# Two-branch long convolution on one core: P rows in two buffers, phases on ScalarE, one reader per PSUM tile, and another order

## The chip, the cores and the metric

The kernel runs on one core of a Trainium2 chip. The metric is the device time of one execution in microseconds. The kernel before took 277.68 us as the median of three runs (277.12 to 280.39). The profile is of one execution of its own, which took 277.69 us; its span from the first to the last recorded instruction is 275.8 us.

The engines are named as in the profile: PE is TensorE (matmuls), PEld its weight loads, DVE is VectorE, ACT is ScalarE, POOL is GpSimd, SP is SyncE, which issues most transfers.

## The reference

L is 2048 positions, D is 448 channels, N is 256 modes. Branch A is a state-space convolution whose kernel K is made from complex exponentials; branch B is a short filter of four taps, a product with v, and a long convolution with a given kernel. The output mixes both branches by a gate g, one number per position.

```python
def _A_ref(u, A_re, A_im, B_re, B_im, C_re, C_im, log_dt, Dskip):
    dt = jnp.exp(log_dt)[:, None]
    ...
    P = jnp.exp(logdA[:, :, None] * l[None, None, :])
    K = jnp.einsum("dn,dnl,dn->dl", Cc, P, dB).real
    ...
    y = irfft2(rfft2(pad(u)) * rfft2(pad(K)))[..., :L]
    return y + u * Dskip

def _B_ref(q, k, v, shift_k, ssm_k, ssm_D):
    ...
    k_shift = k_shift + k_pad[:, t:t + S, :] * shift_k[:, ks - 1 - t]   # t = 0..3
    kv = k_shift * v
    y = irfft2(rfft2(pad(kv)) * rfft2(pad(ssm_k)))[:S] + kv * ssm_D
    return q * y

x = A_u
g = _sigmoid((x * gate_w).sum(-1, keepdims=True))
a = _A_ref(x, A_A_re, A_A_im, A_B_re, A_B_im, A_C_re, A_C_im, A_log_dt, A_Dskip)
b = _B_ref(x, B_k, B_v, B_shift_k, B_ssm_k, B_ssm_D)
return g * a + (1 - g) * b
```

(The transforms are abridged: pad, rfft2 and irfft2 stand for what the reference spells out with axes and types.)

## The kernel before

**Convolution by transforms on TensorE.** Channels go in four chunks H = 0 to 3 of 4 x 28 channels. For each chunk and branch a sequence is brought into transformed form in two steps: `spread` (PSUM tiles ps_c, copied to a tile zs or, for branch A's kernel, zsK) and `transform` (PSUM tiles ps, copied back over zs). `swapped` makes zsS, zs with its two halves of partitions exchanged, by two transfers on SP's queue. `products` multiplies zsS and zs by the transformed kernel on VectorE. `stage_a` (PSUM ps_a, copied to U) and `stage_b` (PSUM ps_b) transform back. Nearly every copy out of PSUM is a ScalarE instruction (`evac`); `evac_two`, used in the last step, gives every second one to VectorE. zs, zsS, zsK, U and others share a pool of NBQ = 7 buffers under the tag "q". Three PSUM buffers "ps" of two banks each serve spread, transform, stage_a and stage_b.

**The kernel K of branch A** is made in eight blocks j = 0 to 7, two per chunk. `Tables.levels` and `Tables.reals` fill a table ET (its parts are called EQ and EP): magnitudes by Exp, phases as integers (ks_ph) by a multiply and add on VectorE, then Sin on ScalarE, a product of the two, and for some entries a negation, on ScalarE for EQ's and on VectorE for EP's. Exp and Sin lie in different table sets, so ScalarE loads a table between them (ACT_TABLE_LOAD). `KGen.q_rows` builds 32 Q rows per chunk (kg_TQ). `KGen.block` builds P rows in the tile kg_TP: rows 0 to 15 by doublings (`mult` into kg_P, `add` back into kg_TP) and rows 16 to 31 as mirrored rows (`back`). For rows 8 to 15 one half of the product is written to kg_TP and the other to kg_P, and a transfer on GpSimd's queue with an accumulate adds them. TensorE then multiplies Q and P rows into the one PSUM tile pk; ScalarE copies it to kg_S; `gather` (PSUM ps_g, copied to kg_KT) puts the taps in order, and spread brings them into zsK.

**The opening.** Modes (A, B, C, four tables) are loaded and multiplied by the step size dt (ks_dt) on TensorE (ps_m). ScalarE copies the exponents into the tile early, where hold keeps, interleaved in one tile per half, two exponents and the coefficients; VectorE makes the coefficients (ks_tC_re, ks_tC_im, early). `save` writes them to memory (xfd), from where each later chunk loads its part (ks_xf). The four taps of branch B run as matmuls of k, transposed while loading, with diagonal matrices (front); VectorE multiplies the result (ps_v) into vt. `stage_b` of the constants fills sb_G in four pieces (phases sb_ph on VectorE, Sin on ScalarE, 16 products on VectorE). `sk_cols` adds dB to the first column of the loaded kernel skraw, on GpSimd.

**The steps.** `step` runs over the sequence B0, B1, A0, B2, A1, none, A2, B3; in each, a new chunk's spread and transform, the former's stage_a and stage_b, and one block. In the end come A's chunk 3, block 7, `mix` (weighings by the gate, gb and og), `transform_half` and `stage_a_half` in halves, and `epilogue_A`, which multiplies by the gate, adds (ept, vt) and stores.

**The order.** No engine call is made when the code meets it. The class Order records each, and `issue` makes them in the order of the list ORDER, each tied behind the one before it on the same engine. So every engine's order is that of the list, while semaphores keep data dependencies. As all are issued by one line, the profile gives nearly everything the same line (L148); groups are told apart by tiles.

```python
    def issue(self):
        last, done = {}, 0
        for run in ORDER.split():
            a, _, b = run.partition("-")
            for f, args, kw in self.calls[int(a):int(b or a) + 1]:
                ins = f(*args, **kw)
                engine = str(ins.ins.engine)
                if engine in last:
                    after(self.tc, ins, last[engine])
                last[engine] = ins
```

Of the kernel before, what the change touches and what calls it, by code (L numbers as in the profile page):

```python
# [9 lines left out]
ACT = mybir.ActivationFunctionType  # L10
ALU = mybir.AluOpType
# [6 lines left out]
P = 128  # L18
# [20 lines left out]
NBQ = 7  # L39
# [312 lines left out]


def transform_half(nc, psum, W, zs, evac, half):
    for kk in range(2):
        pt = psum.tile([P, 2, 512], f32, name="ps_2", tag="ps")
        for i in range(16):
            k = 16 * kk + i
# [686 lines left out]
```

## Time and profile before

| | |
|---|---|
| median of three runs | 277.68 us |
| the profiled execution | 277.69 us |
| its span | 275.8 us |
| granted TensorE clock, mean | 0.956 |
| DVE busy | 241.7 us, 488 instructions |
| ACT busy | 226.7 us, 383 instructions |
| PE busy | 210.7 us, 5770 matmuls |
| POOL busy | 15.9 us |
| transfers | 24.74 MB, mean 90 GB/s |

The page's strip of the span in 40 equal slices, 6.9 us each; a digit is the busy share in tenths:

```profile
PE   0610958879988799798997789867887999699830
DVE  7599899999989799979996899899999997967950
ACT  2795696999899999998998799999999989546400
POOL 8000000000400000100010001001001001000000
PEclk9999999999999899998998999999999999979975
```

A row of a group reads: line, engine, operation, written tile <- read tiles, sizes, count, then busy us, mean ns of one, and the idle time of the engine just before them with what ended it. A row of the timeline reads: start, length, engine, instruction, count, and in brackets how long the engine had been idle and what it waited for. In the table of waits, the numbers are us in total, times, and the longest.

### The profile page before, as it was taken

Reading aid. Unit: us, or ns where it says so; the run is one execution under the profiler, and the core shown is the slowest. Engines: PE = TensorE matmul, PEld = TensorE weight load, DVE = VectorE, ACT = ScalarE, POOL = GpSimd, SP = SyncE. Lnnn points to the kernel's source line nnn. Section 1 sums busy time; section 2 is a strip of 40 time slices with the busy share of each in tenths; the row PEclk is TensorE's granted clock in tenths of the full one; section 3 lists DMA queues with packets and bytes.
Section 4 is the critical chain, followed back from the end, with each engine's and each line's share of the span. In section 5 each row is a group of like instructions: output and inputs, shape, how many; then the busy total and the mean of one; then the engine's idle time right before and its main releaser. Section 6 shows DMA issues by size and latency. Waiting matters only on the chain.

```text
span 275.8 us, 12739 instructions
## 1 busy us (share of the span) xinstructions
PE 210.7 (76%) x5770; PEld 193.3 (70%) x5770; DVE 241.7 (88%) x488; ACT 226.7 (82%) x383; POOL 15.9 (6%) x51
## 2 busy tenths in 40 slices
PE   0610958879988799798997789867887999699830
PEld 0500858877887798687995779766886899688820
DVE  7599899999989799979996899899999997967950
ACT  2795696999899999998998799999999989546400
POOL 8000000000400000100010001001001001000000
PEclk9999999999999899998998999999999999979975
DMA  7999799607804500390093019003042263600077
GB/s 149 224 204 172 131 235 175 99 1 153 118 5 91 116 5 4 83 186 5 5 209 47 5 50 199 10 2 70 6 90 64 54 138 60 147 5 2 2 141 127
DMA packets 55110, 24.74 MB, mean 90 GB/s; under 512 B 49680, under 2 KB 52368, under 8 KB 55056
## 3 DMA queue, kind: packets, MB, share of 16 engines
q1 hardware_dynamic: 48640, 19.34, 37.7%
q0 software_dynamic: 1152, 3.67, 7.2%
q10 hardware_dynamic: 5264, 0.92, 2.1%
q8 instruction: 45, 0.74, 1.2%
q14 instruction: 9, 0.07, 0.1%
HBM read 7.95 MB, written 2.87 MB: 39 GB/s over the span
## 4 chain that ended last, share of the span: by engine, by line
ACT 38%; PE 29%; DVE 15%; DMA 9%; issue 5%; SPq 0%; DVEq 0%; POOL 0%; POOLq 0%; ACTq 0%
ACT zs L148 15%; ACT ET L148 7%; ACT U L148 6%; DMA kg_TP<-kg_P 6%; PE pk L148 5%; PE ps_a L148 5%; PE ps L148 5%; PE ps_c L148 5%; PE ps_b L148 5%; ACT zsK L148 5%; DVE vt L148 2%; DVE scratch L148 2%; PE ps_g L148 2%; PE ps_gate L148 2%; DMA skraw<-in_B_ssm_k_dram 2%
## 5 line engine op out<-in xcount | busy, mean ns | idle before, releaser
L148 ACT CAST zs<-ps 128x896 bf16<-128x896 f32 x48 | 44.0, 944 | 1.0 <-PE ps L148 0.6
L148 ACT CAST zs<-ps_c 128x1024 bf16<-128x1024 f32 (+1 forms) x48 | 42.7, 937 | 1.3 <-PE ps_c L148 1.2
L148 PEld LDWEIGHTS <-front 128*32 128x32 bf16 (+1 forms) x496 | 19.1, 159 | 27.3 <-issue 22.3
L148 PEld LDWEIGHTS <-s_W 128*128 128x128 bf16 x544 | 28.9, 100 | 12.7 <-issue 9.6
L148 PE MATMUL pk<-kg_TP,kg_TQ 128*32 128x32 bf16 x1792 | 33.2, 242 | 5.1 <-issue 2.9
L148 PEld LDWEIGHTS <-kg_TQ 128*32 128x32 bf16 x1792 | 31.2, 160 | 7.0 <-issue 4.8
L148 PE MATMUL ps_a<-sa_R,zs 128*128 128x128 bf16 x224 | 32.7, 235 | 0.3
L148 ACT CAST U<-ps_a 128x1024 bf16<-128x1024 f32 (+1 forms) x30 | 27.2, 936 | 6.9 <-PE ps_a L148 6.7
L148 PE MATMUL ps_b<-U,sb_G 128*128 128x28 bf16 x1024 | 29.5, 175 | 4.1 <-issue 1.4
L148 PE MATMUL ps_a<-sa_R,zsS 128*128 128x128 bf16 x224 | 32.1, 232 | 0.5 <-DVE zsS L148 0.5
L148 PE MATMUL ps<-zs,s_W 128*128 128x112 bf16 x384 | 27.7, 220 | 5.5 <-ACT zs L148 4.2
L148 PEld LDWEIGHTS <-sb_G 128*128 128x128 bf16 x1024 | 27.8, 96 | 5.8 <-issue 3.2
L148 DVE TENSOR_TENSOR kg_TP<-kg_TP,ET 128x1792 bf16<-128x1792 bf16 x24 | 26.1, 1090 | 5.8 <-DMA kg_TP<-kg_P 5.0
L148 PEld LDWEIGHTS <-zsS 128*128 128x128 bf16 x224 | 29.6, 152 | 1.3 <-DVE zsS L148 0.7
L148 PEld LDWEIGHTS <-zs 128*128 128x128 bf16 x224 | 29.4, 151 | 0.8
L148 PE MATMUL ps_v<-front 128*32 128x336 bf16 (+3 forms) x448 | 16.0, 310 | 16.0 <-DVE front L148 13.1
L148 ACT ACTIVATE ET<-ks_ph 128x448 bf16<-128x448 int16 x40 | 23.2, 602 | 4.1 <-DVE kg_P L148 2.6
L148 DVE TENSOR_TENSOR kg_TQ<-kg_TQ,ET 128x896 bf16<-128x896 bf16 (+1 forms) x36 | 24.8, 730 | 0.0
L148 DVE TENSOR_TENSOR kg_P<-kg_TP,ET 128x1792 bf16<-128x1792 bf16 (+1 forms) x24 | 22.4, 934 | 0.1
L148 PE MATMUL ps_c<-Wc,uu 128*64 128x128 bf16 x224 | 18.4, 290 | 1.6 <-ACT U L148 0.6
L148 PE MATMUL ps_c<-Wc,vt 128*64 128x128 bf16 x224 | 17.1, 285 | 1.4 <-ACT zs L148 1.2
L148 PEld LDWEIGHTS <-uu 128*64 128x64 bf16 x224 | 16.5, 210 | 2.4 <-issue 1.5
(102 smaller groups left out, 427.4 us busy)
## 6 DMA issues: line engine op xcount, KB each, us to landing
zsS<-zs SPq DMA_DIRECT2D x16, 448.0 KB, 5.7
kg_TP<-kg_P POOLq DMA_DIRECT2D x8, 448.0 KB, 5.7
vt<-in_B_v_dram SPq DMA_DIRECT2D x4, 448.0 KB, 6.8
skraw<-in_B_ssm_k_dram SPq DMA_DIRECT2D x16, 112.0 KB, 4.8
uu<-in_A_u_dram SPq DMA_DIRECT2D x4, 448.0 KB, 8.5
ks_xf<-xfd SPq DMA_DIRECT2D x3, 336.0 KB, 3.3
out_dram<-vt ACTq DMA_DIRECT2D x8, 112.0 KB, 3.8
out_dram<-vt SPq DMA_DIRECT2D x8, 112.0 KB, 3.6
```

Source lines behind the costliest of these rows:

```text
L148: ins = f(*args, **kw)
```

## The change

The change has these parts:

1. P rows: a tile kg_TP of 48 rows is allocated once. Even blocks use rows 0 to 15 as their first rows, odd blocks rows 32 to 47; the mirrored rows 16 to 31 are shared. Where rows come in another order, matmuls and `gather` read them so; gather has 16 matmuls more. The pool "q" has six buffers for seven; the scratch tile that shares the place of kg_TP grows with it.
2. The last block adds its rows 8 to 15 on VectorE, without the accumulating transfer.
3. Coefficients lie apart from exponents: hold is three tiles' worth of separate ranges; save makes six transfers where it made two.
4. One reader per PSUM tile in `transform_half`: four tiles of one bank, each read by one engine, where two tiles of two banks were each read by both.
5. The phases of the first chunk (ks_ph from early) and those of sb_G (sb_ph) are made on ScalarE by Identity activations with a bias from memory.
6. EQ's negation moves from ScalarE to VectorE; the add of dB moves from GpSimd to VectorE.
7. A new list ORDER. In it ScalarE has 9 table loads for 11.

```diff
-NBQ = 7
+NBQ = 6
...
+        self.turns = {x: self.carve(1).bitcast(f32) for x in (0.0, QUARTER, 8192.0, 8192.0 + QUARTER)}
+        for x, t in self.turns.items():
+            nc.gpsimd.memset(t, x)
...
-                self.phases(ph[:, :, r, :], jv, k_col, o)
+                nc.scalar.activation(ph[:, :, r, :], jv, ACT.Identity, scale=k_col[:, 0:1], bias=o)
...
-    for kk in range(2):
-        pt = psum.tile([P, 2, 512], f32, name="ps_2", tag="ps")
...
-        for i in range(2):
-            k0 = 16 * kk + 8 * i
-            evac(half_of(zs, k0, k0 + 8, half), pt[:, i, 0:448].rearrange("p (k c) -> p k c", c=CB), i)
+    for kk in range(4):
+        pt = psum.tile([P, 512], f32, name="ps_2", tag="ps")
...
+        evac(half_of(zs, 8 * kk, 8 * kk + 8, half), pt[:, 0:448].rearrange("p (k c) -> p k c", c=CB), kk % 2)
...
-        TP = self.pool.tile([P, 32, 2, M], bf16, name="kg_TP")
+        if j == 0:
+            self.TA = self.pool.tile([P, 48, 2, M], bf16, name="kg_TP")
+        TP, late = self.TA[:, 32 * (j % 2):32 * (j % 2) + 16], self.TA[:, 16:32]
+        both = self.TA[:, 16 * (j % 2):16 * (j % 2) + 32]
...
+        if j == NBLK - 1:
+            add(8, mult(TP[:, 0:4], 64))
+            add(12, mult(TP[:, 4:8], 64))
+        else:
+            self.summed(TP[:, 8:16], TP[:, 0:8], EP[:, entry_of(64) - EQ_N + 1], M)
...
-            self.dma.dma_start(self.xfd[:, 4 * i + b:4 * i + 4], t[:, b:4])
+            for k in range(3):
+                self.dma.dma_start(self.xfd[:, 4 * i + b:4 * i + 4, k], t[k][:, b:4])
...
-                V.tensor_scalar(out=o, in0=f, scalar1=e * turn, scalar2=off + (QUARTER if c == first else 0.0),
-                                op0=ALU.mult, op1=ALU.add)
+                shift = off + (QUARTER if c == first else 0.0)
+                if h:
+                    V.tensor_scalar(out=o, in0=f, scalar1=e * turn, scalar2=shift, op0=ALU.mult, op1=ALU.add)
+                else:
+                    nc.scalar.activation(o, f, ACT.Identity, scale=e * turn, bias=self.cons.turns[shift])
...
-                    nc.scalar.mul(B[:, :, 2], B[:, :, 0], -1.0)
+                    V.tensor_scalar(out=B[:, :, 2], in0=B[:, :, 0], scalar1=-1.0, scalar2=None, op0=ALU.mult)
...
-        nc.gpsimd.tensor_tensor(out=raw[:, :, 0], in0=raw[:, :, 0], in1=dB[:, H * NC:(H + 1) * NC], op=ALU.add)
+        V.tensor_tensor(out=raw[:, :, 0], in0=raw[:, :, 0], in1=dB[:, H * NC:(H + 1) * NC], op=ALU.add)
```

The new function `summed` holds what `block` did in place: the two halves of the product and the accumulating transfer.

```python
    def summed(self, dst, src, r, m):
        n = src.shape[1]
        part = self.pool.tile([P, 8 * 2 * M], bf16, name="kg_P4", tag="kg_P4", bufs=2)[:, 0:n * 2 * m]
        for c, out in enumerate((part.rearrange("p (n v m) -> p n v m", n=n, v=2), dst)):
            self.nc.vector.tensor_tensor(out=out, in0=src[:, :, c].unsqueeze(2).to_broadcast([P, n, 2, m]),
...
        self.nc.gpsimd.dma_start(dst.rearrange("p n v m -> p (n v m)"), part, accum_op=ALU.add)
```

More of the change, by code (lines that the diff above doesn't have):

```diff
@@ L354, in transform_half @@
 def transform_half(nc, psum, W, zs, evac, half):
-    for kk in range(2):
-        pt = psum.tile([P, 2, 512], f32, name="ps_2", tag="ps")
-        for i in range(16):
-            k = 16 * kk + i
-            nc.tensor.matmul(pt[:, i // 8, (i % 8) * 56:(i % 8 + 1) * 56], lhsT=W[:, k].rearrange("p r s -> p (r s)"),
-                             rhs=half_of(zs, k, k + 1, half), start=True, stop=True)
-        for i in range(2):
-            k0 = 16 * kk + 8 * i
-            evac(half_of(zs, k0, k0 + 8, half), pt[:, i, 0:448].rearrange("p (k c) -> p k c", c=CB), i)
+    for kk in range(4):
+        pt = psum.tile([P, 512], f32, name="ps_2", tag="ps")
+        for i in range(8):
+            nc.tensor.matmul(pt[:, i * 56:(i + 1) * 56], lhsT=W[:, 8 * kk + i].rearrange("p r s -> p (r s)"),
+                             rhs=half_of(zs, 8 * kk + i, 8 * kk + i + 1, half), start=True, stop=True)
+        evac(half_of(zs, 8 * kk, 8 * kk + 8, half), pt[:, 0:448].rearrange("p (k c) -> p k c", c=CB), kk % 2)
 def stage_a_half(nc, psum, U, R, terms, evac, half):
@@ L424, in add @@
         self.nc.vector.tensor_tensor(out=T[:, rows].rearrange("p n v m -> p (n v) m"), in0=v[:, :, 0], in1=v[:, :, 1], op=ALU.add)
+    def summed(self, dst, src, r, m):
[3 more added lines that the diff above has]
+            self.nc.vector.tensor_tensor(out=out, in0=src[:, :, c].unsqueeze(2).to_broadcast([P, n, 2, m]),
+                                         in1=bass.AP(r.tensor, r.offset + c * m, [list(r.ap[0]), [0, n], [-m, 2], [1, m]]), op=ALU.mult)
+        self.nc.gpsimd.dma_start(dst.rearrange("p n v m -> p (n v m)"), part, accum_op=ALU.add)
     def q_rows(self):
@@ L469, in back @@
             src = bass.AP(lo.tensor, lo.offset + (15 - i0) * 2 * M, [list(lo.ap[0]), [-2 * M, i1 - i0], [M, 2], [1, M]])
-            V.tensor_tensor(out=TP[:, 16 + i0:16 + i1], in0=src,
+            V.tensor_tensor(out=late[:, i0:i1], in0=src,
                             in1=EP[:, E_R - EQ_N + i0:E_R - EQ_N + i1].unsqueeze(2).to_broadcast([P, i1 - i0, 2, M]), op=ALU.mult)
@@ L477, in block @@
         add(4, mult(TP[:, 0:4], 32))
-        part = self.pool.tile([P, 8, 2 * M], bf16, name="kg_P4", tag="kg_P4", bufs=2)
-        r = EP[:, entry_of(64) - EQ_N + 1]
-        for c, out in enumerate((part.rearrange("p n (v m) -> p n v m", v=2), TP[:, 8:16])):
-            V.tensor_tensor(out=out, in0=TP[:, 0:8, c].unsqueeze(2).to_broadcast([P, 8, 2, M]),
-                            in1=bass.AP(r.tensor, r.offset + c * M, [list(r.ap[0]), [0, 8], [-M, 2], [1, M]]), op=ALU.mult)
-        nc.gpsimd.dma_start(TP[:, 8:16].rearrange("p n c m -> p (n c m)"), part.rearrange("p n x -> p (n x)"), accum_op=ALU.add)
+        if j == NBLK - 1:
[3 more added lines that the diff above has]
+            self.summed(TP[:, 8:16], TP[:, 0:8], EP[:, entry_of(64) - EQ_N + 1], M)
         back(8, 16)
@@ L492, in block @@
                         m = (hf * 4 + g) * CB + hw
-                        r0 = TP[:, 0, c, m:m + 1]
-                        rhs = bass.AP(r0.tensor, r0.offset, [list(r0.ap[0]), [32 * M + (1 - 2 * c) * M, 2], [2 * M, 16]])
+                        d = c ^ (j % 2)
+                        r0 = both[:, 0, d, m:m + 1]
+                        rhs = bass.AP(r0.tensor, r0.offset, [list(r0.ap[0]), [32 * M + (1 - 2 * d) * M, 2], [2 * M, 16]])
                         nc.tensor.matmul(pt[32 * g:32 * g + NQ, hw, :].rearrange("p (i j) -> p i j", i=2),
@@ L524, in gather @@
                         s0 = 0 if kind == "last" else 8 * a0 + b1[0] + (kind == "next")
-                        n = len(b1)
-                        out = o[32 * a0:32 * a0 + 32, b1[0]:b1[-1] + 1:st, :] if n > 1 else o[32 * a0:32 * a0 + 32, b1[0], :]
-                        rhs = S[:, s0:s0 + (n - 1) * st + 1:st, :] if n > 1 else S[:, s0, :]
-                        jobs.append((a0, out, cons.col_of(key), rhs))
+                        first = b1[0]
+                        for b1 in ([b for b in b1 if j % 2 == 0 or s0 + b - b1[0] < 16], [b for b in b1 if j % 2 and s0 + b - b1[0] >= 16]):
+                            if not b1:
+                                continue
+                            s1, n = (s0 + b1[0] - first + 16 * (j % 2)) % 32, len(b1)
+                            out = o[32 * a0:32 * a0 + 32, b1[0]:b1[-1] + 1:st, :] if n > 1 else o[32 * a0:32 * a0 + 32, b1[0], :]
+                            rhs = S[:, s1:s1 + (n - 1) * st + 1:st, :] if n > 1 else S[:, s1, :]
+                            jobs.append((a0, out, cons.col_of(key), rhs))
             if r == 0:
@@ L534, in gather @@
                     jobs[jobs.index(x)] = x + (i == 0, i == len(mine) - 1)
-            for a0, out, lhsT, rhs, first, last in jobs:
-                nc.tensor.matmul(out, lhsT=lhsT, rhs=rhs, start=first, stop=last, tile_position=(0, 32 * a0))
+            for a0, out, lhsT, rhs, begin, end in jobs:
+                nc.tensor.matmul(out, lhsT=lhsT, rhs=rhs, start=begin, stop=end, tile_position=(0, 32 * a0))
             if r % 4 == 3:
@@ L548, in __init__ @@
         self.dt = dt
-        self.hold = [early[:, 4096 + 1344 * i:5440 + 1344 * i].bitcast(f32).rearrange("p (b t m) -> p b t m", b=4, t=3) for i in range(2)]
+        part = lambda i, t: early[:, 4096 + 1344 * i + 448 * t:4544 + 1344 * i + 448 * t].bitcast(f32).rearrange("p (b m) -> p b m", b=4)
+        self.hold = [[part(i, t) for t in range(3)] for i in range(2)]
         for c, nm in enumerate(("A_re", "A_im")):
@@ L552, in __init__ @@
             for i, t in enumerate(self.hold):
-                nc.scalar.copy(self.by_block(t[:, :, c]), self.nat(pt[:, :, 0:448], i))
+                nc.scalar.copy(self.by_block(t[c]), self.nat(pt[:, :, 0:448], i))
     @staticmethod
@@ L564, in low @@
     def low(t, c):
-        return t[:, :, 2].bitcast(bf16)[:, :, c * M:(c + 1) * M]
+        return t.bitcast(bf16)[:, :, c * M:(c + 1) * M]
     def wide(self, nm, timed):
@@ L591, in coefficients @@
             of = lambda n, c: self.nat(prod[n][:, c], i)
-            V.tensor_tensor(out=self.by_block(self.low(t, 0)), in0=of(0, 0), in1=of(1, 1), op=ALU.add)
-            V.tensor_tensor(out=self.by_block(self.low(t, 1)), in0=of(0, 1), in1=of(1, 0), op=ALU.subtract)
+            V.tensor_tensor(out=self.by_block(self.low(t[2], 0)), in0=of(0, 0), in1=of(1, 1), op=ALU.add)
+            V.tensor_tensor(out=self.by_block(self.low(t[2], 1)), in0=of(0, 1), in1=of(1, 0), op=ALU.subtract)
     def save(self):
@@ L614, in levels @@
         if h == 0:
-            xf = self.hold[0][:, 0:nb]
+            xf = [t[:, 0:nb] for t in self.hold[0]]
         else:
-            xf = self.pool.tile([P, nb, 3, M], f32, name="ks_xf")[:]
-            self.dma.dma_start(xf, self.xfd[:, nb * h:nb * h + nb])
-        f, exps = xf[:, :, 1], self.exps
-        self.x = xf[:, :, 0]
+            ld = self.pool.tile([P, nb, 3, M], f32, name="ks_xf")[:]
+            self.dma.dma_start(ld, self.xfd[:, nb * h:nb * h + nb])
+            xf = [ld[:, :, t] for t in range(3)]
+        f, exps = xf[1], self.exps
+        self.x = xf[0]
         turn = 65536.0 / (2.0 * math.pi)
@@ L666, in levels @@
         for c in range(2):
-            V.tensor_tensor(out=p4[:, :, c], in0=self.low(xf, c).unsqueeze(1).to_broadcast([P, 2, nb, M]),
+            V.tensor_tensor(out=p4[:, :, c], in0=self.low(xf[2], c).unsqueeze(1).to_broadcast([P, 2, nb, M]),
                             in1=p0.rearrange("p b a m -> p a b m"), op=ALU.mult)
@@ L760, in body @@
     nc.scalar.dma_start(ldt[:], A_log_dt.rearrange("(g l) -> l g", g=4))
-    cons = Consts(nc, wp, kgp.tile([P, 3584], i32, name="scratch", tag="kg_TP"))
+    cons = Consts(nc, wp, kgp.tile([P, 5376], i32, name="scratch", tag="kg_TP"))
     cons.rows()
@@ L827, in body @@
     tb = Tables(nc, kgp, qt, hqt, psum, raw, ident, dt, xfd, nc.sync, early)
+    tb.cons = cons
     tb.coefficients()
```

137 rows, old and new, of the table ORDER are left out of this document.

## The prediction

> **What bounds the kernel now.** I read the busy times by engine first, then the chain of waits, then the busy time by stretch, and last the order in time of ScalarE and VectorE at both ends. Engines and chain:
>
> ```profile
> PE 210.7 (76%) x5770; PEld 193.3 (70%) x5770; DVE 241.7 (88%) x488; ACT 226.7 (82%) x383; POOL 15.9 (6%) x51
> ACT 38%; PE 29%; DVE 15%; DMA 9%; issue 5%; SPq 0%; DVEq 0%; POOL 0%; POOLq 0%; ACTq 0%
> ```
>
> VectorE (DVE) is the busiest, but ScalarE (ACT) is most often the link that ended last. Stretches say why (columns: length, then PE, PEld, DVE, ACT, POOL, granted clock, DMA, GB/s):
>
> ```profile
> 0.00:28.00 28.00, 5.45 (x52) 4.82 (x56) 23.32 (x93) 17.62 (x40) 5.96 (x39) 1.00 1.12 187
> 28.00:48.00 20.00, 16.68 (x472) 15.12 (x465) 18.84 (x49) 15.70 (x23) 0.71 (x2) 1.00 1.02 180
> 48.00:230.00 182.00, 158.46 (x4318) 145.28 (x4318) 170.72 (x313) 174.35 (x296) 8.33 (x9) 0.97 0.35 69
> 230.00:276.00 46.00, 30.14 (x935) 28.09 (x933) 28.86 (x36) 19.01 (x26) 0.85 (x1) 0.84 0.38 72
> ```
>
> So there are three stages. In the opening VectorE is full (42.2 of 48 us) and ScalarE has 14.7 us of holes. From 48 to 230 ScalarE is full (174.35 of 182). In the end neither is: work goes from hand to hand. ScalarE in the opening:
>
> ```profile
> 8.60 0.54 ACT L148 COPY early<-ps_m 128x448 f32<-128x448 f32 x1 [3.98 <-PE ps_m L148]
> 9.47 1.49 ACT L148 ACTIVATE ET<-early 128x224 bf16<-128x224 f32 x5
> ...
> 22.12 2.44 ACT L148 ACTIVATE ET<-ks_ph 128x448 bf16<-128x448 int16 x5 [1.44 <-DVE ks_ph L148]
> ...
> 28.66 0.40 ACT L148 ACTIVATE ET<-early 128x224 bf16<-128x224 f32 x1 [2.41 <-DVE early L148]
> ...
> 44.98 0.58 ACT L148 ACTIVATE ET<-ks_ph 128x448 bf16<-128x448 int16 x1 [2.57 <-DVE kg_P L148]
> 45.58 1.28 ACT L148 ACT_TABLE_LOAD   x1
> ```
>
> Each hole waits for VectorE; after the last load, at 46.86, ScalarE's long full stretch begins. Five 224-wide activations take 1.49 us, so one adds 0.28, about 0.10 less than its 386 ns alone. Below I use such steps (mean less 0.10) for both engines; added up they give ScalarE 179.8 us between that load and the copy kg_S of block 6 at 225.34, which lasted 178.5, so there it has no slack at all.
>
> All sums are against this execution: span 275.8 and 1.9 around it, 277.69; the median shown is 277.68.
>
> **The opening, part by part.** The rows that price it:
>
> ```profile
> L148 DVE TENSOR_SCALAR ks_ph<-early 128x224 int32<-128x224 f32 x20 | 4.5, 267 | 3.0 <-ACT early L148 3.0
> L148 DVE TENSOR_SCALAR sb_ph<-scratch,sb_offs 128x512 int32<-128x512 int32 x8 | 5.1, 633 | 0.2
> L148 ACT ACTIVATE ET<-early 128x224 bf16<-128x224 f32 x16 | 5.5, 386 | 2.4 <-DVE early L148 2.4
> L148 ACT ACT_TABLE_LOAD x11 | 14.1, 1283 | 2.9 <-issue 2.8
> ```
>
> *Phases.* VectorE loses 20 + 8 instructions, 9.6 us. ScalarE gains 28 Identity activations, a form this trace does not have. Low bound, the step of the Exp row (0.29) and of the 512-wide copy from PSUM (617 ns, so 0.52): 20 x 0.29 + 8 x 0.52 = 9.9 us. High bound, no overlap and 0.04 us of gap: 20 x 0.43 + 8 x 0.66 = 13.9. They cannot be below the low bound, since the step of a plain Exp of that width already is. I take 12, the middle, because each reads a bias (eight a scale too) from memory and no row shows what that costs.
>
> Here a page weighs in. The Trainium skill, "ScalarE: Activation LUTs", section "What ACT_TABLE_LOAD costs", gives 186 ns + 0.833 ns per element, about 93 ns more for each operand read through a pointer, and 93 ns of overlap. By it the 28 would take an estimated 20 x 0.37 + 8 x 0.71 = 13.1 us, and the end would be 1.1 us later than I forecast. The same page's "Rules for kernel authors" wants multiply and add on VectorE, not ScalarE; this trace agrees as to length (267 against 386 ns), not as to who is short of time.
>
> *Loads and signs.* The changed order has 9 table loads for 11, both gone from the opening: -2.57. The first chunk's three negations of ET leave ScalarE for VectorE: -1.4 (2 x 0.54 + 0.34). One Exp and one magnitude go ahead of the last load or behind it; nothing. *Start.* ks_dt moves to the head of VectorE's order (it was done there at 7.4 behind phases), needing only the Exp that ended at 4.62; cast 0.17, ks_dt 0.73 and ps_m 1.1 give a first copy at 6.6, not 8.60.
>
> Sum: ScalarE's steps to the end of the last load go from 31.95 to 37.3 (low), 39.4 (taken), 41.3 (high). Before, 1.5 us of them lay ahead of 8.60. From 6.6: 6.6 + 39.4 - 1.5 = 44.5, and 0.9 for holes that remain: 45.4 against 46.86, **-1.5** (low and no holes -4.4; high with 2 us of holes +1.5). The holes go because VectorE's steps up to the eighth vt product fall from 41.6 to 33.5, and because hold in three tiles lets magnitudes be read while coefficients are written (the 2.41 above). What is late next is ScalarE itself.
>
> *At nothing.* The add of dB moves from GpSimd to VectorE, 4 x 0.15; the first now stops VectorE until skraw has landed, with the last vt product, sixteen sb_G products and block 0's rows queued behind it. Saving hold takes six transfers for two, some 4 x 0.4 = 1.6 us of SP's queue, and the first now waits there for ScalarE's copies of early; behind it stand gw, skraw, ks_xf and the uu loads. Before, skraw let GpSimd go at 39.29 and TensorE used it at 46.5; 41 is still in time, and if it weren't, each us late is a us. Sixteen more matmuls in gather cost 16 x 0.04 on TensorE, which has 23.5 us free in the middle. The order around the rest of the opening is covered by ScalarE.
>
> **The middle (to kg_S of block 6).** ScalarE loses nine negations, 6 x 0.54 + 3 x 0.34 = 4.3, and by the two orders gains 0.6 of other work (three U copies of 1024 come in, three zsK of 896 go out): 179.8 to 176.2. VectorE takes on the nine (its own negations take 274 ns, so 1.4 to 2.3) and three adds of dB, and hands the gate's small steps and two 1792-wide weighings to the end: 170.0 to 168.9. P rows in two buffers let block j+1's first rows be written while TensorE still reads block j's; the waits this removes are small (1.4 us, below), the freedom of order is the rest. I take **-3.3**; bounds -3.65 and 0, if holes eat it.
>
> ```profile
> DVE kg_TP L148 <- DMA kg_TP<-kg_P: 5.0, 3, 2.1
> DVE kg_TP L148 <- PE pk L148: 1.4, 2, 0.8
> SPq L148 <- PE ps_a L148: 20.5, 4, 8.0
> ```
>
> The accumulating transfer stays for seven blocks; its 5.0 us of waits get no credit, as ScalarE sets this stage.
>
> **The end.** From 225.2, where block 7's rows begin, VectorE needs 32.7 us of steps but 41.0 of time, to 266.23; then 9.6 of output transfers and closing, unchanged. Its holes:
>
> ```profile
> 233.55 2.02 DVE L148 TENSOR_TENSOR zsS<-zsS,zsK 128x3584 bf16<-128x3584 bf16 x1 [1.95 <-ACT zsK L148]
> 249.32 0.62 DVE L148 CAST kg_KT<-ps_g 128x448 bf16<-128x448 f32 x1 [3.37 <-PE ps_g L148]
> 253.57 0.54 ACT L148 CAST zsK<-ps 128x448 bf16<-128x448 f32 x1 [1.52 <-DVE zsK L148]
> ```
>
> Block 7 loses its transfer for a product less, a product more and two adds of 896 (0.64 each): +1.3. Its rows then take 9.8 us of steps, not 11.6 of time. One reader per PSUM tile removes the 1.52. With the weighings and gate steps VectorE now has 37.4 us here: mostly filler for those holes. I take 39.6 (2.2 of holes): **-1.4**; bounds 37.4 (-3.6) and 45.8 (no hole filled, +4.8).
>
> Sum: -1.5 - 3.3 - 1.4 = -6.2; span 269.6, and 1.9: **271.5 us**. Bounds together: 266.0 to 284.0.
>
> **Rivals.** *ScalarE pays all back in the opening:* the 28 activations at 13.9 and 2 us of holes, +1.5 for -1.5: 274.5. For it: ScalarE becomes the opening's only full engine. Against: 7.4 us of its holes there (the last three shown and one of 0.97) waited for VectorE. By the page's price this lies nearer. *Everything fits:* low price, saturated middle, 1 us of holes at the end: -4 - 3.6 - 2.6, 267.5. For it: ScalarE had no slack in the middle on the old order either. *The new order only trades stalls:* one swap exposed (next), 277.2.
>
> *Slower: six buffers instead of seven.* The swap zsS<-zs writes into a q buffer and takes a median 5.7 us to land; with one buffer less it starts later, products on VectorE wait, and ScalarE's PSUM copies behind them. For it: SP already sat 20.5 us waiting for ps_a to free such buffers. Against: no product waited for a swap, only 2.7 us for zsK. Each of seven fully exposed costs 5.7; one eats the gain (6.2), two (11.4) fall just short of 6.2 + 5.6, so it is slower by 2% from the third on: 271.5 + 17.1 = 288.6.
>
> **Chances.** 2% (5.6 us) is about what can be told from no change: below 272.1 is faster, above 283.2 slower. Forecast 0.48, three quarters of it below 272.1, as it sits so near; everything fits 0.12; paid back 0.20; traded stalls 0.08; slower 0.12. So faster 0.36 + 0.12 = 0.48, same 0.12 + 0.20 + 0.08 = 0.40, slower 0.12. Range 266 to 280: it takes in the first four and leaves about 0.15 out, nearly all above.
>
> **What would show it.** Identity rows on ScalarE at 0.3 to 0.43 us a step; first ps_m copy near 6.6; last opening load ending near 45.4; kg_S of block 6 near 220.5; no zsK copy waiting for VectorE at the end; VectorE's last product near 260. Swap transfers named as what VectorE waits for, or ScalarE with more than 10 us of holes in the middle, would prove me wrong.

## The result, and the profile after

| | before | after |
|---|---|---|
| median, four runs each, side by side | 278.75 us (277.12 to 280.39) | 269.54 us (268.57 to 271.26) |
| the profiled execution | 277.69 us | 271.26 us |
| its span | 275.8 us | 269.5 us |

The ratio is 0.968, 95% interval 0.959 to 0.976. The forecast was 271.5. One thing to keep in mind before any term is read: the profiled execution of after is the slowest of its four and that of before lies 1.1 us under the median. The two traces therefore differ by 6.4 us where the medians differ by 9.2.

Busy times by engine, and the chain of waits, from the page of after:

```profile
PE 214.8 (80%) x5786; PEld 194.9 (72%) x5786; DVE 237.4 (88%) x478; ACT 231.8 (86%) x397; POOL 11.8 (4%) x50
...
ACT 51%; PE 23%; DVE 15%; issue 5%; DMA 1%; DVEq 0%; ACTq 0%
```

DMA fell from 9% of the chain to 1%, and ScalarE's share of it rose from 38% to 51%. The kernel now hangs on ScalarE's order more, and on transfers less. The same by stretches (length, then PE, PEld, DVE, ACT, POOL, granted clock, DMA, GB/s):

```profile
0.00:28.00 28.00, 9.99 (x142) 8.44 (x146) 18.22 (x69) 22.17 (x55) 5.58 (x43) 1.00 1.06 176
28.00:48.00 20.00, 14.16 (x386) 12.79 (x379) 17.71 (x47) 19.31 (x29) 0.00 (x0) 0.83 1.00 169
48.00:224.00 176.00, 161.33 (x4349) 146.24 (x4349) 172.31 (x328) 170.68 (x290) 6.17 (x7) 0.96 0.38 74
```

In the opening ScalarE has filled up (41.5 of 48 us, before 33.3) while VectorE went from 42.2 to 35.9. In the middle VectorE is busy for 172.31 of 176 us (165.44 before) and ScalarE for 170.68 (168.35 before). The opening on ScalarE, as its timeline shows it (start, length, and in brackets the idle time before and its cause):

```profile
4.64 0.21 ACT L149 ACTIVATE scratch<-ldt 112x4 bf16<-112x4 bf16 x1 [2.17 <-DMA ldt<-in_A_log_dt_dram]
7.14 0.54 ACT L149 COPY early<-ps_m 128x448 f32<-128x448 f32 x1 [2.29 <-PE ps_m L149]
...
30.25 0.26 ACT L149 ACTIVATE scratch<-scratch 128x64 bf16<-128x64 int16 x1 [0.50 <-DVE scratch L149]
...
45.43 1.28 ACT L149 ACT_TABLE_LOAD   x1
```

From 7.14 on there is one hole, of 0.50. Of the holes that waited for VectorE only this one is left, and still the last load ends at 46.71, where before it ended at 46.86. What filled the time are these groups (count | busy us, mean ns | idle before):

```profile
L149 ACT ACT_TABLE_LOAD x9 | 11.5, 1283 | 1.3 <-PEq L1052 1.2
...
L149 ACT ACTIVATE ks_ph<-early,scratch 128x224 int32<-128x224 f32 x20 | 8.5, 470 | 0.1
L149 ACT ACTIVATE sb_ph<-scratch,sb_offs 128x512 int32<-128x512 int32 x8 | 6.4, 807 | 0.0
```

The end, on VectorE:

```profile
235.67 0.63 DVE L149 CAST kg_KT<-ps_g 128x448 bf16<-128x448 f32 x1 [2.79 <-PE ps_g L149]
...
247.99 0.63 DVE L149 TENSOR_TENSOR zsS<-zsS,zsK 128x896 bf16<-128x896 bf16 x1 [1.16 <-ACT zsK L149]
...
258.92 0.39 DVE L149 TENSOR_TENSOR vt<-ept,vt 128x448 bf16<-128x448 bf16 x1
```

No zsK copy on ScalarE waits for VectorE any more. The milestones, from the timelines of the two traces:

| | before | after | forecast |
|---|---|---|---|
| first ps_m copy starts | 8.60 | 7.14 | 6.6 |
| last load of the opening ends | 46.86 | 46.71 | 45.4 |
| kg_S of block 6 starts | 225.34 | 219.86 | 220.5 |
| the middle (the difference of the two) | 178.48 | 173.15 | 175.2 |
| VectorE's last product ends | 266.23 | 259.31 | about 260 |
| from there to the end of the span | 9.6 | 10.2 | 9.6 |

### The profile page after: what moved, and what is told of

The parts are those of the page before. It is cut to its first block, busy times and chain, and to the rows that moved or that the text cites. A ratio compares the mean times of both kernels' runs of the same rounds, so it can differ in the third digit from the quotient of the medians.

```text
span 269.5 us, 12769 instructions
## 1 busy us (share of the span) xinstructions
PE 214.8 (80%) x5786; PEld 194.9 (72%) x5786; DVE 237.4 (88%) x478; ACT 231.8 (86%) x397; POOL 11.8 (4%) x50
## 4 chain that ended last, share of the span: by engine, by line
ACT 51%; PE 23%; DVE 15%; issue 5%; DMA 1%; DVEq 0%; ACTq 0%
ACT zs L149 19%; ACT ET L149 9%; PE ps L149 5%; PE ps_b L149 5%; ACT U L149 5%; PE pk L149 4%; PE ps_c L149 4%; ACT zsK L149 4%; ACT sb_ph L149 3%; ACT L149 2%; ACT ks_mag L149 2%; PE ps_a L149 2%; ACT kg_KT L149 2%; DVE kg_TP L149 2%; DVE early L149 2%
## 5 line engine op out<-in xcount | busy, mean ns | idle before, releaser
L149 PEld LDWEIGHTS <-front 128*32 128x32 bf16 (+1 forms) x496 | 20.5, 159 | 26.5 <-issue 19.0
L149 PE MATMUL pk<-kg_TP,kg_TQ 128*32 128x32 bf16 x1792 | 35.9, 241 | 4.2 <-issue 3.4
L149 PEld LDWEIGHTS <-s_W 128*128 128x128 bf16 x544 | 30.7, 104 | 7.5 <-issue 4.7
L149 PE MATMUL ps_b<-U,sb_G 128*128 128x28 bf16 x1024 | 30.8, 176 | 4.3 <-issue 1.6
L149 PE MATMUL ps_a<-sa_R,zsS 128*128 128x128 bf16 x224 | 31.0, 228 | 0.1
L149 PE MATMUL ps_v<-front 128*32 128x224 bf16 (+3 forms) x448 | 17.9, 325 | 13.6 <-DVE front L149 6.3
L149 DVE TENSOR_TENSOR kg_TP<-kg_TP,ET 128x1792 bf16<-128x1792 bf16 x23 | 24.8, 1082 | 0.2 <-ACT ET L149 0.2
L149 ACT ACTIVATE ET<-ks_ph 128x448 bf16<-128x448 int16 x40 | 24.5, 632 | 0.1
L149 ACT CAST zsK<-ps_c 128x512 bf16<-128x512 f32 (+3 forms) x27 | 17.5, 653 | 4.3 <-PE ps_c L149 4.3
L149 DVE TENSOR_TENSOR kg_P<-kg_TQ,ET 128x1792 bf16<-128x1792 bf16 (+1 forms) x20 | 17.8, 897 | 1.0 <-DMA kg_TP<-kg_P 1.0
```

## The experiments

They ran in four groups, each on one chip with the kernel before beside it: a0 to a3; a4 to a6 and b1; b2, c1 and c2; a7. The medians of the kernel before in them were 278.2, 278.2, 278.3 and 277.9 us. Each was timed five rounds. Names that begin with a are the changed kernel with one thing undone, b the kernel before with one part of the change alone, c the changed kernel taken further. Differences are against a0, the changed kernel in the first group. By the ratios, which set each run against the kernel before on its own chip, they are +18.4, +11.3, +4.3, +3.8, +0.7, +4.7 and +0.6 us for a1 to a7, -0.6 for c1 and -2.1 for c2.

| run | median, us | ratio to before, 95% | against a0 |
|---|---|---|---|
| a0, the changed kernel | 269.21 | 0.969 (0.964 to 0.975) | |
| a1, five parts undone, order kept | 287.98 | 1.036 (1.030 to 1.041) | +18.8 |
| a2, negations on ScalarE | 281.13 | 1.010 (1.007 to 1.014) | +11.9 |
| a3, ks_ph on VectorE | 273.61 | 0.985 (0.980 to 0.989) | +4.4 |
| a4, sb_ph on VectorE | 273.57 | 0.983 (0.978 to 0.988) | +4.4 |
| a5, two readers per tile | 270.65 | 0.972 (0.967 to 0.977) | +1.4 |
| a6, last block by transfer | 274.90 | 0.986 (0.981 to 0.992) | +5.7 |
| a7, dB on GpSimd | 270.20 | 0.972 (0.966 to 0.977) | +1.0 |
| b1, negations, old order | 279.15 | 1.003 (1.000 to 1.006) | |
| b2, sb_ph, old order | 276.76 | 0.995 (0.992 to 0.998) | |
| c1, phases in a hole | 269.20 | 0.967 (0.963 to 0.971) | 0.0 |
| c2, c1 and earlier vt | 268.17 | 0.962 (0.958 to 0.966) | -1.0 |

**a0: the changed kernel again.** No edit.

> The changed kernel itself, as the mark for the others of this set. It took 269.54 us; both theories expect 269 to 271 and the kernel before at 278 to 279.

269.21 us (267.73 to 271.38), and its profiled execution of 269.24 sits at that median: span 267.4, last opening load ending at 46.69, kg_S of block 6 at 219.10. It is the trace that the next runs are compared with.

**a1: five parts undone, the order kept.** Phases on VectorE, EQ's negations on ScalarE, the dB add on GpSimd, two readers per tile at the end:

```diff
-                nc.scalar.activation(ph[:, :, r, :], jv, ACT.Identity, scale=k_col[:, 0:1], bias=o)
+                self.phases(ph[:, :, r, :], jv, k_col, o)
...
-        pt = psum.tile([P, 512], f32, name="ps_2", tag="ps")
+        if kk % 2 == 0:
+            both = psum.tile([P, 2, 512], f32, name="ps_2", tag="ps")
+        pt = both[:, kk % 2]
...
-                if h:
-                    V.tensor_scalar(out=o, in0=f, scalar1=e * turn, scalar2=shift, op0=ALU.mult, op1=ALU.add)
-                else:
-                    nc.scalar.activation(o, f, ACT.Identity, scale=e * turn, bias=self.cons.turns[shift])
+                V.tensor_scalar(out=o, in0=f, scalar1=e * turn, scalar2=shift, op0=ALU.mult, op1=ALU.add)
...
-                    V.tensor_scalar(out=B[:, :, 2], in0=B[:, :, 0], scalar1=-1.0, scalar2=None, op0=ALU.mult)
+                    nc.scalar.mul(B[:, :, 2], B[:, :, 0], -1.0)
...
-        V.tensor_tensor(out=raw[:, :, 0], in0=raw[:, :, 0], in1=dB[:, H * NC:(H + 1) * NC], op=ALU.add)
+        nc.gpsimd.tensor_tensor(out=raw[:, :, 0], in0=raw[:, :, 0], in1=dB[:, H * NC:(H + 1) * NC], op=ALU.add)
```

> The changed kernel with its order, its two buffers of P rows, its six buffers q and its separate coefficients, but with the 28 phases back on VectorE, the 12 negations back on ScalarE, the adds of dB back on GpSimd, and two readers per PSUM tile at the end. Theory (ScalarE's work sets the middle): the negations cost ScalarE 5.7 us of steps again, the two readers 1.5, and the phases give about nothing either way, so 275 to 277, with some 3 left for order and buffers. Rival (order and buffers bring the gain, the five edits are small change): 269 to 271.5.

287.98 us: both accounts missed, by more than 10 us. The new order, with its row buffers, its split coefficients and the last block on VectorE, is slower than the old kernel once the moved steps stand on their old engines. In its trace the last load of the opening ends 5.6 us later than in a0, the middle takes 8.5 us more and what follows 3.0. TensorE's granted clock was lower (0.918, in a0 0.959), but its busy time rose by only 2.4 us (215.4 for 213.0), so the clock explains little of it. So the order is no gain of its own on top of which the parts add theirs; it is an order for these parts. The next runs take them one at a time; the sum of their differences, 23.1, is more than 18.8, so the parts overlap.

**a2: EQ's negations on ScalarE again.** The fourth piece of the diff above, alone.

> The changed kernel with the 12 negations of EQ back on ScalarE. Theory (ScalarE has no slack from the opening to block 6): 12 steps, 8 x 0.54 + 4 x 0.34 = 5.7 us more on ScalarE, so 4 to 5.7 above the changed kernel. Rival (they fall into holes): within 1.

+11.9 us, twice what the 12 negations cost in steps. The table of waits in the middle (48 to 224 us; us in total, times, longest) names where the other half went:

```profile
DVE kg_P L149 <- ACT ET L149: 10.1, 4, 5.8
```

In a0's table of the same stretch no kg_P waits for ET. The worst of the four, on VectorE's timeline:

```profile
201.00 0.63 DVE L149 TENSOR_TENSOR kg_P<-ET 128x896 bf16<-128x896 bf16 x1 [5.78 <-ACT ET L149]
```

ScalarE's timeline, with the negation that it waited for and what came of it:

```profile
200.35 0.61 ACT L149 ACTIVATE ET<-ET 128x448 bf16<-128x448 bf16 x1
...
224.75 3.48 ACT L149 CAST U<-ps_a 128x1024 bf16<-128x1024 f32 x4 [7.63 <-PE ps_a L149]
```

The negation itself lasts 0.61, but on ScalarE it stands behind PSUM copies of U and zs. VectorE, whose next instruction needs it, stops for 5.78, and the Q rows that it was making come late. The table of waits on TensorE from 195 to 226 us has them:

```profile
PE pk L149 <- DVE kg_TQ L149: 5.2, 1, 5.2
```

The matmuls ps_a are queued behind those of pk, and ScalarE waits 7.63 for ps_a (2.46 in a0). A step on the wrong side of a hand-over is paid twice.

**a3: the 20 early phases on VectorE again.** The third piece of the diff, alone.

> The changed kernel with the 20 phases of the first chunk back on VectorE. ScalarE loses 20 x 0.37 = 7.4 us of steps in the opening, VectorE gains 20 x 0.17 to 0.23 = 3.4 to 4.5. Theory A (ScalarE's new work sets the opening): 3 to 6 us faster than the changed kernel. Theory B (VectorE's eighth vt product, at 48.2, sets it as well, and VectorE is full from 15.4 on): 1 to 3 us slower.

+4.4 us, with 7.4 us of steps taken off ScalarE. Its timeline:

```profile
16.73 1.28 ACT L149 ACT_TABLE_LOAD   x1
26.05 2.01 ACT L149 ACTIVATE ET<-ks_ph 128x448 bf16<-128x448 int16 x4 [8.04 <-DVE ks_ph L149]
31.11 0.58 ACT L149 ACTIVATE ET<-ks_ph 128x448 bf16<-128x448 int16 x1 [2.31 <-DVE ks_ph L149]
```

ScalarE reaches its Sin table 5.7 us earlier and then stands 8.04 and 2.31 us for phases; the last load starts at 48.09 instead of 45.41. VectorE is nearly full from about 15 us on, so it is a bound of the opening as ScalarE is.

**a4: the eight phases of sb_G on VectorE again.** The first piece of the diff, alone.

> The changed kernel, with the eight phases sb_ph (128x512) back on VectorE. ScalarE steps fall by 8 x 0.71 = 5.7 us, VectorE's rise by 8 x 0.53 = 4.3. Theory (VectorE fills the opening of the changed kernel as much as ScalarE, as the return of the small phases showed with +4.4 us): the last opening load comes 1 to 3 us later than 46.7, total +1 to +5 us. Rival (ScalarE alone sets the opening, the forecast's account): -3 to -5 us.

+4.4 us again: theory met by its total, rival out. ScalarE's timeline has the holes, and a last load 3.8 us later than in a0, where 1 to 3 were expected:

```profile
37.27 1.06 ACT L149 ACTIVATE sb_ph<-sb_ph 128x1024 bf16<-128x1024 int16 x1 [4.43 <-DVE sb_ph L149]
48.12 1.08 ACT L149 ACTIVATE sb_ph<-sb_ph 128x1024 bf16<-128x1024 int16 x1 [2.58 <-DVE sb_ph L149]
49.22 1.28 ACT L149 ACT_TABLE_LOAD   x1
```

**a5: two readers per PSUM tile again.** The second piece of the diff, alone.

> The changed kernel, with transform_half's four PSUM tiles of one bank joined again to two of two banks, each read by ScalarE and VectorE. Theory (the forecast's: one reader per tile removes a wait of 1.5 us at the end): a zsK copy waits again 1 to 1.5 us for VectorE and the total rises by 1 to 1.5 us. Rival (ScalarE there waits for the matmuls in any case, by 1.6 and 0.9 us in the changed kernel): 0 to +0.4.

+1.4 us by the medians, +0.7 by the ratios, whose intervals overlap: not told from nothing. The traces do not tell it either. VectorE's wait for zsK, 0.47 us in a0, is 1.67 in a5:

```profile
246.32 0.63 DVE L149 TENSOR_TENSOR zsS<-zsS,zsK 128x896 bf16<-128x896 bf16 x1 [1.67 <-ACT zsK L149]
```

But with one reader per tile the same wait lasted 0.70 in a7, 0.73 in a6 and 1.16 in after. From kg_S of block 6 to VectorE's last product a5 took 39.2 us, between the 38.2 of a7 and the 39.5 of after (a0 38.5). The wait that the theory named, of a zsK copy on ScalarE for VectorE, did not come back: these copies wait for matmuls alone (2.6 us, as in after). So what this part is worth under the new order stays open.

**a6: the last block by the accumulating transfer again.**

```diff
-            add(8, mult(TP[:, 0:4], 64))
-            add(12, mult(TP[:, 4:8], 64))
+            V.memset(self.pool.tile([P, 1], bf16, name="kg_none")[:], 0.0)
+            self.summed(TP[:, 8:16], TP[:, 0:8], EP[:, entry_of(64) - EQ_N + 1], M)
```

> The changed kernel, with rows 8 to 15 of the last block summed by the accumulating transfer again, as in the other blocks. VectorE does 1.3 us less, and its next instruction waits for the transfer, 2 us or a little more from issue to landing. Theory (the last block stands alone on VectorE, nothing to put into that wait): +1 to +3 us, with a hole of 2 us or more before kg_P in block 7. Rival (the end waits for TensorE's ps_g in any case and the 2.8 us hole there takes it up): 0 to +0.5.

+5.7 us, above both. The memset of one element only keeps the count of calls for the list. The hole is there on VectorE's timeline, three times as long as I had put it:

```profile
225.59 1.09 DVE L149 TENSOR_TENSOR kg_TP<-kg_TP,ET 128x1792 bf16<-128x1792 bf16 x1 [6.21 <-DMA kg_TP<-kg_P]
```

This transfer took 6.6 us from issue to landing, and the new order has nothing on VectorE to put beside it. The 2 us that I expected fit the longest wait for such a transfer in the kernel before (2.1), not its landing, for which the page of before has a median of 5.7. From kg_S of block 6 to VectorE's last product a6 took 43.7 us, a0 38.5. The 2.9 us wait for ps_g that the rival trusted to take it up stays as long as it was.

**a7: the dB add on GpSimd again.** The last piece of the diff, alone.

> The changed kernel, with the four adds of dB (128x28) on GpSimd again: 4 x 0.85 us there, 4 x 0.15 us of steps off VectorE. Theory (the forecast put this move at nothing, as the first add finds skraw landed and VectorE has filler around it): -0.5 to +0.5 us. Rival (a step that one more engine hands on adds its own latency where TensorE waits for skraw: 0.6 us at the end of the opening already): +0.5 to +2 us, PE ps_c waiting over 1 us for POOL skraw at 46 to 48.

+1.0 us, with intervals that overlap: not told from nothing. The rival's mechanism is not in the trace, rather its opposite. GpSimd adds at 39.00, long before TensorE comes at 45.72; in a0, with the add on VectorE, TensorE waits 0.61 us for it and starts at 46.85. Neither shows further on: ScalarE's first copy of that result starts at 48.19, in a0 at 48.13, held by its own last load.

**b1: the negations on VectorE, in the kernel before.**

```diff
-                    nc.scalar.mul(B[:, :, 2], B[:, :, 0], -1.0)
+                    V.tensor_scalar(out=B[:, :, 2], in0=B[:, :, 0], scalar1=-1.0, scalar2=None, op0=ALU.mult)
```

> The kernel before in its own order, with one edit alone: the 12 negations for EQ go from ScalarE to VectorE. ScalarE loses 8 x 0.54 + 4 x 0.34 = 5.7 us of steps, VectorE gains 2 to 3. Theory A (the part is worth its steps, ScalarE having no slack in the middle): -3 to -5 us, ratio 0.982 to 0.99. Theory B (the part is worth something only where the order suits it, since undoing it under the new order cost 11.9 us, twice its steps): -1 to +3 us, with VectorE waiting for ET's Sin and product, and ScalarE waiting for PSUM copies behind it.

279.15 against 278.2: nothing, theory B. Two lines tell it, the stretch from 48 to 224 us in the kernel before and in b1 (columns as above):

```profile
48.00:224.00 176.00, 152.46 (x4148) 139.44 (x4151) 165.44 (x305) 168.35 (x288) 8.33 (x9) 0.97 0.35 69
```

```profile
48.00:224.00 176.00, 153.68 (x4132) 140.42 (x4132) 166.32 (x316) 165.42 (x280) 8.27 (x9) 0.94 0.35 68
```

ScalarE's busy time fell by 2.9 us (fourth pair) and its idle time grew by as much. From the end of the last load (48.30, 1.4 us later than before) to kg_S of block 6 it was 179.05 us, before 178.48. ScalarE is the busiest there and still not what its steps alone decide.

**b2: the phases of sb_G on ScalarE, in the kernel before.**

```diff
-                self.phases(ph[:, :, r, :], jv, k_col, o)
+                nc.scalar.activation(ph[:, :, r, :], jv, ACT.Identity, scale=k_col[:, 0:1], bias=o)
```

> The kernel before in its own order, with one edit alone: the eight phases sb_ph (128x512) go from VectorE to ScalarE, 8 x 0.71 = 5.7 us of steps there, 5.1 us fewer on VectorE. Under the new order the same edit is worth 4.4 us. Theory A (the edit is worth something by itself, since ScalarE has 14.7 us of holes there that wait for VectorE): last opening load 1 to 4 us before 46.86, total -1 to -4 us. Theory B (like the negations, it is worth nothing without an order made for it): 0 to +4 us, ScalarE's added steps delaying the Sins that VectorE waits for.

276.76 us, ratio 0.995 (0.992 to 0.998): theory A by its total, at its low end, but not by its place, as the last load ends only 0.3 us earlier (46.58). Alone this part is worth 1.5 us, where undoing it under the new order costs 4.4.

**c1: twelve early phases in VectorE's hole.** VectorE waits 5.1 us for ps_m ahead of ks_tC_im (a0, 10.3 to 15.4). Twelve phases go there; in the list their calls stand right behind the copy of early that they read.

```diff
-                if h:
+                if h or e in (-124.0, -256, 16, -512, 32, 64):
                     V.tensor_scalar(out=o, in0=f, scalar1=e * turn, scalar2=shift, op0=ALU.mult, op1=ALU.add)
```

> The changed kernel, with 12 of its 20 early phases ks_ph on VectorE, and not at their old places but in the 4.5 to 5.1 us in which VectorE waits for ps_m ahead of ks_tC_im (from 10.3 to 15.4). ScalarE loses 12 x 0.37 = 4.4 us of steps, VectorE's 12 x 0.27 = 3.2 us lie in a hole; ks_b is copied 1.5 us earlier. Theory (both engines bound the opening, so a phase may go to VectorE only where that waits): the last load ends 1 to 4 us before 46.7, the total is 1 to 4 us under the changed kernel's 269.2, that is ratio 0.953 to 0.965. Rival (the chain over vt and TensorE sets the opening's end, its first vt product staying near 33): 0 to -0.5 us, ScalarE waiting for ps_c after its load instead.

269.20 us, no gain: the rival's total, though not by the wait that it named. ScalarE's timeline says where 4.4 us of steps went:

```profile
19.26 1.28 ACT L150 ACT_TABLE_LOAD   x1
29.29 0.26 ACT L150 ACTIVATE scratch<-scratch 128x64 bf16<-128x64 int16 x1 [3.65 <-DVE scratch L150]
44.48 1.28 ACT L150 ACT_TABLE_LOAD   x1
```

The first Sin load came 3.2 us earlier, then ScalarE stood 3.65 us for a small step of VectorE, and the last load was 0.9 earlier. The phases did fit the hole (12 of them in 2.31 us from 10.65). ScalarE then copies ps_c from 47.19 on without a wait for TensorE. At kg_S of block 6 the trace is 1.0 us ahead of a0's, which the medians do not show.

**c2: c1, and the first two vt products earlier on VectorE.** Only the list differs from c1: calls 131 and 416, with TensorE's ps_v calls that must come before and behind them (103-130 move up behind 388-415), go ahead of six steps of VectorE, and ga_sel (959, 960) goes behind. An excerpt of the list, written without its line breaks:

```diff
-845 866 959-960 869-871 2126 60 103-130 884 912 918 1508 131 910 474-501 59 850 539 61 416 502-530 913 901 874-875 951 556
+845 866 131 474-501 416 502-529 869-871 2126 60 884 912 918 1508 910 59 850 539 61 530 913 901 874-875 951 959-960 556
```

> As the run before, and on VectorE's order the first two vt products stand ahead of six small or later-needed steps (ET products of the last levels, kg_P of block 0, and ga_sel behind them), so that TensorE, which stood 5.2 us for DVE vt, goes on 3 to 4 us earlier. Theory (ScalarE and the vt chain are the two bounds of the opening): -3 to -4.5 us against 269.2, ratio 0.950 to 0.959, with PE ps_v waiting 1 to 2 us for vt and the first ps_c matmuls near 43. Rival (v lands only near 32 to 34, so that vt cannot start earlier): no better than the run before, with VectorE now standing for DMA vt.

268.17 us. The forecast for it failed, and its rival's mechanism shows in VectorE's timeline:

```profile
32.71 2.09 DVE L150 TENSOR_TENSOR vt<-ps_v,vt 128x896 bf16<-128x896 f32 x2 [1.95 <-DMA vt<-in_B_v_dram]
```

v has not landed before 32.7. TensorE went on at 33.86 (c1 34.46, a0 35.42), and lost it again waiting for the add of dB, which the change moved to VectorE:

```profile
45.88 1.98 PE L150 MATMUL ps_c<-Wc,skraw 128*64 128x128 bf16 x40 [2.03 <-DVE skraw L150]
```

c1 had reached this point at 45.24. Neither time decides: ScalarE's last load ends at 45.78, as in c1 (45.76), behind the same wait of 3.7 us for VectorE's small step, and its first copy of ps_c, at 47.22, does not wait for TensorE. So the landing of v keeps the vt chain from starting earlier (the 16 DMA engines are busy throughout, with shares of 1.08 and 1.00 in c2's windows from 0 to 28 and 28 to 48); that it bounds the opening is not shown. c2 has the lowest median of all, but its interval (0.958 to 0.966) overlaps that of a0 (0.964 to 0.975), so that it beats the changed kernel isn't shown.

Not run: one buffer for the P rows or seven "q" buffers under the new order, and six "q" buffers under the old one. So parts 1 and 3 have no price of their own here, nor has the list of part 7 apart from them.

## Why the prediction came out right

The sum was -6.2 us and the two profiled traces differ by 6.3 in their spans. That is luck: against the forecast the opening came out 1.35 us worse and the closing 0.6, and the middle 2.0 better.

**The opening: the activations were mis-sized, and ScalarE isn't its only bound.** Forecast -1.5, measured -0.15. The first copy came 0.54 later than I had it, as the Exp ahead of it waited 2.17 us for the transfer of log_dt and ended at 4.85 rather than 4.62, and the cast behind it took 0.55 rather than 0.17. The 28 activations, at 470 and 807 ns, take 20 x 0.37 + 8 x 0.71 = 13.1 us by my own way of counting steps, not the 12 that I took. Holes are 0.5, not 0.9. Together -1.5 + 0.5 + 1.1 - 0.4 = -0.3, where -0.15 was measured. Taking the middle between two ends was the slip, with no row for what a bias or a scale read from memory costs. The price that fits stood beside the sum: by the Trainium skill, "ScalarE: Activation LUTs", section "What ACT_TABLE_LOAD costs", 186 ns + 0.833 ns per element and about 93 ns per pointer operand, an estimate is 466 ns for 224 elements with one such operand and 799 for 512 with two. The trace agrees within about 1%. There is a slip in the sum too: 31.95 + 12 - 2.57 - 1.4 is 40.0, not 39.4. The 0.6 fit the Exp and the magnitude (2 x 0.29) that the text puts at nothing; in the trace of after four Exps stand behind the last load, in that of before one.

Worse than the size is the sentence "What is late next is ScalarE itself". In this trace it was true, but it made ScalarE look like the only lever. a3 and a4 take 7.4 and 5.7 us off ScalarE and make the kernel slower by 4.4, c1 takes off 4.4 and gains nothing. Close behind it stands VectorE, nearly full from 15 us on: as soon as ScalarE has fewer steps, it waits for VectorE (8.04 us in a3, 4.43 in a4, 3.65 in c1). The vt chain on TensorE is near as well, reaching ps_c at 46.9 in a0, but in a0, c1 and c2 ScalarE does not wait for it.

**The middle: right in sign, too small, and its reason fell.** Forecast -3.3 with bounds of -3.65 and 0; measured -5.3 in the trace of after, outside them. Four more traces run the same program up to block 6 or differ from it there by little (a0, a5, a6, a7): 172.4, 171.7, 170.4 and 173.5 us for before's 178.5, that is -5.0 to -8.1. The step that failed is "there it has no slack at all". I had added ScalarE's steps up to 179.8 us for a stretch of 178.5 and read this as saturation, so that a step less is as much time less. But the row of the stretch from 48 to 230 had ScalarE busy for 174.35 of 182 us, so 7.65 us were idle, and the sum of steps hid them. b1 takes the same negations away under the old order, and the time stays. The windows say what the order does with the negations gone from ScalarE: in the same 176 us it is busy 2.3 us longer than before (170.68 for 168.35), and VectorE 6.9 (172.31 for 165.44). So the middle gained by steps taken off and by idle time closed on both engines. The second I had called "the freedom of order" and given nothing. How the gain splits between the two is not shown. The accumulate waits, which got no credit, shrank from 5.0 to 1.0 us in this trace (1.6 in a0); no run tells how much of the gain is theirs.

**The end: -1.4, as forecast; the parts of it were not.** From kg_S of block 6 to VectorE's last product 39.45 us, before 40.89; in a0 38.49. One reader per tile was to give 1.5; the wait of ScalarE for VectorE is gone, but a5 doesn't tell its worth from nothing. That block 7 is summed on VectorE I priced at 1.3 us of steps more and 1.8 us of time less (9.8 for 11.6). Under the new order it is worth 5.7 (a6; 4.7 by the ratios), as there the transfer of 6.6 us has nothing beside it. Closing, forecast unchanged, took 0.6 longer in this trace.

**At nothing.** Right as far as it can be told: moving the dB add back is +1.0 with overlapping intervals, and the six saves cost nothing that shows on ScalarE. The reason given for the add fell, though. On VectorE it stands behind most of the vt products and ended at 46.7 in after, not near 41, and TensorE waited for it in other traces (0.61 us in a0, 2.03 in c2). By the forecast's rule each such us would have been a us. It was not, as ScalarE started to copy ps_c later still.

**The rivals.** Six buffers did not bite: the table of waits of after has no wait of VectorE for a transfer into zsS. "Pays all back", with +1.5 in the opening, lay about as far from the measured -0.15 as the forecast with -1.5; of the total it was wrong, since the middle gave more. "Everything fits", at 267.5, lies as near to the median as the forecast, but it rested on the low price of the activations, and they cost more than the middle one. "The order trades stalls" is refuted as a whole by the result. In a1 it is what happens: the new order without the moved steps costs 9.8 us against before.

**The median.** 9.2 us, not 6.4, because the trace of after is of an execution 1.7 us above its median and that of before 1.1 below its own. The granted clock does not explain the first: the slowest and the fastest of the four executions of after have the same 0.930. a0's trace, at its median, differs from before's by 8.4 in span, nearly all of it in the middle and at the end.

## What to carry to other kernels

Where each engine's order is fixed by hand, the price of a moved instruction need not be its duration: it is who waits behind it on two queues, so the same 12 negations were worth nothing in one order and 11.9 us in the other. A part should be priced together with the order it comes with, and "engine X is full" should be tested by taking steps away, not by adding steps up. Before a stage's gain is booked to one engine, look for the chain that ends close behind it; here 4.4 to 7.4 us taken off ScalarE in the opening brought nothing or cost 4.4, as VectorE stood there.

## What the runs showed of the hardware

- An accumulating transfer of 448 KB by GpSimd's queue took 6.6 us to land in a6, where the page of after has a median of 4.8 for its seven and that of before 5.7 for its eight.
- An activation whose bias is read from memory took 470 ns for 224 elements, an Exp of the same width with none 380 (the ET<-early rows of after): 90 ns more (its output is wider too, int32 for bf16).
- The middle took 170.4, 171.7, 172.4 and 173.2 us in four profiled executions whose programs hardly differ up to there (a6, a5, a0, after), and a wait near the end 0.47 to 1.16 us in four that are alike there (a0, a7, a6, after). A term of one or two us can't be read from a pair of traces of this kernel.
